# Stage one of a Strassen-style MoE layer: product 1 summed in product 0's PSUM bank, and the products in the order 0, 5, 1, 6, 3, 4, 2

## The chip, the cores and the metric

The program runs on one core of a Trainium2 chip. The metric is the device time of the whole program in microseconds (us). The core has engines that each work through their own list of instructions in order: TensorE (PE, with its weight loads listed apart as PEld), VectorE (DVE), ScalarE (ACT) and GpSimd (POOL); SyncE (SP) here only issues DMA transfers. They meet through semaphores: an instruction that must wait for another engine holds up everything behind it on its own engine.

## The reference

Sparse attention comes first, then a layer of 8 dense experts on its output:

```python
    B, H, S, D = attn_out.shape                      # 4, 8, 768, 64
    x = np.ascontiguousarray(attn_out.transpose(0, 2, 1, 3)).reshape(B * S, H * D)
...
    N, D = x.shape                                   # 3072, 512
    E = w_gate.shape[1]                              # 8
    logits = x @ w_gate
    logits = logits - logits.max()
    P = np.exp(logits)
    for _ in range(8):
        P /= P.sum(1, keepdims=True) + 1e-09
        P /= P.sum(0, keepdims=True) + 1e-09
        P *= N / E
    out = np.zeros((N, D), dtype=np.float32)
    for e in range(E):
        h = np.maximum(x @ w1[e], 0.0)               # w1[e]: 512 x 1024
        ye = h @ w2[e]                               # w2[e]: 1024 x 512
        out += P[:, e:e + 1] * ye
```

The attention masks blocks of 32 keys, takes exp and sum of each row of scores and multiplies by V. The change touches only `x @ w1[e]`.

## The kernel before

The attention fills about the first 420 us. From there on the kernel works through 32 items, one for each pair of an expert e and a batch b of 768 tokens (i = 4e + b). An item has two stages.

**Stage one** (`stage1(i, qi)`) computes relu(x w1) by a Strassen-like scheme: the two token halves (384 tokens), the two halves of the inner dimension and the two halves of F give four blocks of output, and seven products of prepared sums of blocks take the place of eight. An item has four units, qi = 0 to 3, each 128 rows of F in each half; there are 128 units in all. A product is six matmuls of 128x384 in f16 (two K tiles, each as high x high, high x low, low x high, so that the weights of its third matmul are the first that are read from the low half), and they accumulate in one PSUM bank, `p0` to `p6`, of a pool `ps_h` with four banks. `HDOWN` takes out a scale.

In a unit the products came in the order 0, 1, 5, 6, 3, 4, 2:

- Product 0 is copied to SBUF as `a1` by ScalarE (L1247).
- `comb` (L1212) is a VectorE operation that reads one product from PSUM and adds an SBUF tile: `r11` = product 1 + `a1`, then `a1` += product 5, `u3` = product 6 + `a1`, `c21` = product 3 + `u3`, `u3` += product 4, `a1` += product 4, and `a1` += product 2. Those are seven `comb` in a unit.
- ScalarE makes the relu of `r11` in place (L1252), of `u3` (L1272), of `a1` (L1277) and of `c21` (L1285).
- GpSimd makes the sums that stage two needs as its operands: `s1` = `a1` + `u3` (L1280), then three differences into `a1`, `r11` and `c21` (L1086).
- `emit` turns each of the seven operands into two f16 halves: the high one by ScalarE (L1221), the low one by VectorE or GpSimd (L1226, L1232), which waits for the high one. The pairs are the tiles `h`.

**Stage two** (`stage2(i, p)`, products in the order 1, 0, 5, 6, 3, 4, 2) has three steps for each of its seven products; a step is 12 matmuls of 128x256 (L1332, PSUM tile `py`) and a VectorE update of the output `acc` (L1356).

**What sets the order.** The main loop writes stage two of item i between the products of stage one of item i+1: three steps first, the other 18 spread over the 28 products, one step or none after each. `tick` tells a queue (`Slots`) what each piece costs, and the queue puts delayed work in between: the halves of `h`, the GpSimd sums, and the preparation of weights. A scheduler of the framework, which simulates the engines, then settles the order of each engine's list. Item 0's stage one has no stage two beside it.

**The switch of experts.** In the last unit of an expert's last batch (i = 3, 7, ... 27, qi = 3), every product, once it has been issued for the last time, starts the preparation of the next expert's weights in its place (`split_w1`, the `used` callback): ScalarE writes the high half (L1064), VectorE the low half (L1068). The seven weight tiles lie in the memory areas `arena` (products 0, 1, 5) and `attic` (6, 3, 4, 2), and the splits come in the order 0, 1, 6, 5, 3, 4, 2. The seven switches lie at about 641, 861, 1082, 1302, 1523, 1743 and 1963 us.

The loads of the next item's x (`load_x`) go out on SP for the products in the order 0, 1, 5, 6, 3, 4, 2, before and after the change. The changed function with what calls it, lines as in the profile of before:

Of the kernel before, what the change touches and what calls it, by code (L numbers as in the profile page):

```python
# [9 lines left out]
F32 = mybir.dt.float32  # L10
# [5 lines left out]
AF = mybir.ActivationFunctionType  # L16
# [4 lines left out]
P = 128  # L21
# [8 lines left out]
HDOWN = 2.0 ** -20  # L30
# [24 lines left out]
def tile_sparse_attention_moe(  # L55
# [11 lines left out]
    nc = tc.nc  # L67
    B, H, S, D = q.shape
    NT, DM = out.shape
    NE, _, FF = w1.shape  # L70
# [10 lines left out]
    KH = KD // 2  # L81
    FH = FF // 2
    CH = NC // 2
    TH = S // 2
# [866 lines left out]
    ps_h = mpool("ps_h", 4, space=PSUM)  # L951
# [133 lines left out]
    def sub(out, x, y):  # L1085
        nc.gpsimd.tensor_tensor(out=out, in0=x, in1=y, op=ALU.subtract)  # L1086
# [104 lines left out]
    def stage1(i, qi, used=None):  # L1191
        fs = slice(qi * P, (qi + 1) * P)
        lop = LOPE if i < NLE else LOP

        def product(p):
            slots.need(("w1", i // B, p))
            ps = ps_h.tile([P, 512], F32, tag="ph", name=f"p{p}_{i}_{qi}")[:, :TH]
            for kc in range(KH):
                for m, (l, r) in enumerate(((0, 0), (0, 1), (1, 0))):
                    nc.tensor.matmul(  # L1200
                        ps, lhsT=w1p[p][:, l, kc, fs], rhs=xp[p][:, r, kc],
                        start=(kc == 0 and m == 0), stop=(kc == KH - 1 and m == 2),
                    )
            if used and p in used:
                used[p]()
            return ps

        def fresh(nm):
            return upool.tile([P, TH], F32, tag="u", name=f"{nm}_{i}_{qi}")

        def comb(t, ps, other):
            nc.vector.scalar_tensor_tensor(  # L1212
                out=t, in0=ps, scalar=HDOWN, in1=other, op0=ALU.mult, op1=ALU.add
            )

        def emit(p, src, relu=False, delay=0):
            key = ("h", i, p), i, qi

            def high():
                h = hs[i, p, qi] = hfree.pop(0)  # L1220
                nc.scalar.activation(h[:, 0], src, AF.Relu if relu else AF.Copy)  # L1221

            def low():
                h = hs[i, p, qi]
                if relu:
                    nc.vector.scalar_tensor_tensor(  # L1226
                        out=h[:, 1], in0=src, scalar=0.0, in1=h[:, 0],
                        op0=ALU.max, op1=ALU.subtract,
                    )
                else:  # L1230
                    eng = nc.gpsimd if p in lop else nc.vector
                    eng.tensor_tensor(out=h[:, 1], in0=src, in1=h[:, 0], op=ALU.subtract)  # L1232

            if delay:
                slots.add(high, key, delay, act=0.52)
            else:
                high()
            if p in lop:
                slots.add(low, key, delay, pool=0.95)
            else:  # L1240
                slots.add(low, key, delay + 1, dve=0.6 if relu else 0.78)

        def tick(n, m):
            slots.tick(0.976, 0.55 * n, 0.5 * m)

        a1 = fresh("a1")
        nc.scalar.activation(a1, product(0), AF.Copy, scale=HDOWN)  # L1247
        tick(0, 1)
        yield
        r11 = fresh("r11")  # L1250
        comb(r11, product(1), a1)
        nc.scalar.activation(r11, r11, AF.Relu)  # L1252
        emit(0, r11)
        tick(1, 2)
        yield
        comb(a1, product(5), a1)
        tick(1, 0)
        yield
        u3 = fresh("u3")
        comb(u3, product(6), a1)  # L1260
        tick(1, 0)
        yield
        slots.settle(i, qi - 1)
        c21 = fresh("c21")
        comb(c21, product(3), u3)
        emit(1, c21, relu=True)
        tick(1, 1)
        yield
        p5 = product(4)
        comb(u3, p5, u3)  # L1270
        comb(a1, p5, a1)
        nc.scalar.activation(u3, u3, AF.Relu)  # L1272
        emit(3, u3)
        tick(2, 2)
        yield
        comb(a1, product(2), a1)
        nc.scalar.activation(a1, a1, AF.Relu)  # L1277

        def add():
            nc.gpsimd.tensor_tensor(out=s1, in0=a1, in1=u3, op=ALU.add)  # L1280
            sub(a1, a1, r11)
            slots.need((("h", i, 0), i, qi))
            sub(r11, s1, r11)
            slots.need((("h", i, 1), i, qi))
            nc.scalar.activation(c21, c21, AF.Relu)  # L1285
            sub(c21, c21, r11)

        s1 = fresh("s1")
        slots.add(add, (("sum", i), i, qi), 1, act=0.52, pool=4.3)
        emit(4, s1, delay=SD[0])  # L1290
        emit(6, a1, delay=SD[1])
        emit(5, r11, delay=SD[2])
        emit(2, c21, delay=SD[3])
        tick(1, 1)
        yield
# [94 lines left out]
    def run(steps):  # L1390
        for _ in steps:
            pass

    run(stage1(0, 0))
    for part in split_w2(0, wr[2]):
        part()
    for qi in range(1, FH // P):
        run(stage1(0, qi))
# [6 lines left out]
    def products(i):  # L1405
        e, b = divmod(i, B)
        for qi in range(FH // P):
            swap = qi == FH // P - 1 and b == B - 1 and e + 1 < NE
            yield from stage1(i, qi, split_w1(e + 1) if swap else None)
# [79 lines left out]
```

## Time and profile before

| what | value |
|---|---|
| median of 3 runs | 2212.83 us (2211.21 to 2213.3) |
| the profiled execution's own time | 2212.46 us |
| its span, first to last instruction | 2210.7 us |
| mean granted TensorE clock | 0.997 |
| PE busy | 2159.4 us (98%) |
| DVE busy | 1741.3 us (79%) |
| ACT busy | 1317.0 us (60%) |
| POOL busy | 1334.8 us (60%) |

The profile is one execution, recorded instruction by instruction. A row of the timeline has the start in us, the duration in us, the engine, the line of the kernel, the operation, the tile it writes and the tiles it reads (without the numbers in their names), the shape, and how many instructions run together; square brackets at its end give the idle time ahead of it on its engine and what ended that. Neighbouring matmuls overlap: the start of the next row, not the end of this one, says when the engine was free. The chain of waits follows the work that ended last back through what released it. The table of waits lists the idle time of an engine by what ended it: total us, number of times, longest.

### The profile page before, as it was taken

Reading aid. Unit: us, or ns where it says so; the run is one execution under the profiler, and the core shown is the slowest. Engines: PE = TensorE matmul, PEld = TensorE weight load, DVE = VectorE, ACT = ScalarE, POOL = GpSimd, SP = SyncE. Lnnn points to the kernel's source line nnn. Section 1 sums busy time; section 2 is a strip of 40 time slices with the busy share of each in tenths; the row PEclk is TensorE's granted clock in tenths of the full one; section 3 lists DMA queues with packets and bytes.
Section 4 is the critical chain, followed back from the end, with each engine's and each line's share of the span. In section 5 each row is a group of like instructions: output and inputs, shape, how many; then the busy total and the mean of one; then the engine's idle time right before and its main releaser. Section 6 shows DMA issues by size and latency. Waiting matters only on the chain.

```text
span 2210.7 us, 47146 instructions
## 1 busy us (share of the span) xinstructions
PE 2159.4 (98%) x18892; PEld 1599.2 (72%) x18892; DVE 1741.3 (79%) x2989; ACT 1317.0 (60%) x2443; POOL 1334.8 (60%) x1369
## 2 busy tenths in 40 slices
PE   6999999889999999999999999999999999999999
PEld 3777767657777777777777777777777777777777
DVE  7888999778877768876887688768876887688765
ACT  6988889765567556654565455545554555455442
POOL 3123455595578556855686568656865686567553
PEclk9999999999999999999999999999999999999999
DMA  7667866413121212121212121212121212121221
GB/s 169 139 134 160 210 124 145 128 65 118 51 89 51 89 51 89 51 89 51 89 51 89 51 89 51 89 51 89 51 89 51 89 51 89 51 89 58 79 79 51
DMA packets 195344, 192.35 MB, mean 87 GB/s; under 512 B 132124, under 2 KB 150580, under 8 KB 195124
## 3 DMA queue, kind: packets, MB, share of 16 engines
q1 hardware_dynamic: 194560, 189.30, 31.0%
q8 instruction: 148, 2.42, 0.4%
q14 instruction: 72, 0.59, 0.1%
q10 hardware_dynamic: 564, 0.03, 0.0%
HBM read 140.54 MB, written 17.30 MB: 71 GB/s over the span
## 4 chain that ended last, share of the span: by engine, by line
PE 77%; DVE 10%; ACT 4%; POOL 4%; issue 3%; DMA 1%; SPq 0%; DVEq 0%; POOLq 0%; ACTq 0%
PE py L1332 33%; PE p L1200 33%; PE u L760 3%; PE t L705 2%; PE t L702 2%; PE m L669 2%; PE m L672 2%; DVE top L678 2%; DVE a L1212 1%; DVE attic L1068 1%; POOL s L1280 1%; DVE h L1232 1%; DVE u L1212 1%; ACT h L1221 1%; DVE pl L721 1%
## 5 line engine op out<-in xcount | busy, mean ns | idle before, releaser
L1332 PE MATMUL py<-w2p,h 128*128 128x256 f16 x8064 | 972.9, 273 | 3.8 <-DVE h L1226 1.3
L1332 PEld LDWEIGHTS <-h 128*128 128x128 f16 x8064 | 788.8, 98 | 154.9 <-issue 3.2
L1232 POOL TENSOR_TENSOR h<-u,h 128x384 f16<-128x384 f32 x128 | 128.4, 1003 | 534.8 <-ACT h L1221 534.7
L1200 PE MATMUL p<-attic 128*128 128x384 f16 x2304 | 422.9, 327 | 8.4 <-DVE attic L1068 2.5
L1200 PEld LDWEIGHTS <-attic 128*128 128x128 f16 x3072 | 299.5, 98 | 178.3 <-issue 7.9
L1200 PE MATMUL p<-arena 128*128 128x384 f16 x2304 | 414.8, 326 | 1.4 <-DVE a L1212 0.9
L1356 DVE SCALAR_TENSOR_TENSOR acc<-py,spare,acc 128x256 f32<-128x256 f32 (+1 forms) x588 | 298.7, 514 | 98.6 <-PE py L1332 94.0
L1221 ACT ACTIVATE h<-c 128x384 f16<-128x384 f32 x256 | 131.5, 518 | 344.4 <-DVE c L1212 302.6
L1200 PEld LDWEIGHTS <-arena 128*128 128x128 f16 x2304 | 225.5, 98 | 126.5 <-issue 2.9
L1212 DVE SCALAR_TENSOR_TENSOR a<-p,a 128x384 f32<-128x384 f32 x384 | 211.1, 550 | 17.8 <-PE p L1200 5.0
L1232 DVE TENSOR_TENSOR h<-s,h 128x384 f16<-128x384 f32 x128 | 112.8, 881 | 135.4 <-ACT h L1221 135.3
L678 DVE TENSOR_REDUCE top<-m 128x1 f32<-128x768 f32 x192 | 181.8, 951 | 32.4 <-PE m L672 31.9
L710 ACT ACTIVATE pe<-t,qk 128x768 int32<-128x768 f32 x192 | 171.9, 898 | 46.3 <-PE t L705 43.3
L1086 POOL TENSOR_TENSOR c<-c,r 128x384 f32<-128x384 f32 x128 | 161.2, 1259 | 10.0
L1280 POOL TENSOR_TENSOR s<-a,u 128x384 f32<-128x384 f32 x128 | 138.1, 1079 | 37.0 <-ACT a L1277 36.2
L1086 POOL TENSOR_TENSOR r<-s,r 128x384 f32<-128x384 f32 x128 | 153.5, 1200 | 10.0
L1221 ACT ACTIVATE h<-r 128x384 f16<-128x384 f32 x256 | 128.0, 514 | 51.5 <-POOL r L1086 50.6
L1232 POOL TENSOR_TENSOR h<-r,h 128x384 f16<-128x384 f32 x128 | 146.4, 1144 | 2.6 <-ACT h L1221 2.0
L1200 PE MATMUL p<-arena,attic 128*128 128x384 f16 x768 | 146.4, 326 | 0.9 <-DVE a L1212 0.9
L669 PE MATMUL m<-kt,qt 128*128 128x512 f16 (+1 forms) x384 | 127.1, 331 | 9.3 <-DMA kt<-ks 6.8
L1086 POOL TENSOR_TENSOR a<-a,r 128x384 f32<-128x384 f32 x128 | 128.7, 1005 | 10.0
L702 PE MATMUL t<-qt,kt 128*128 128x512 f16 (+1 forms) x384 | 126.5, 329 | 6.2 <-DVE top L678 5.3
(205 smaller groups left out, 3635.3 us busy)
## 6 DMA issues: line engine op xcount, KB each, us to landing
arena<-xd SPq DMA_DIRECT2D x128, 384.0 KB, 3.4
attic<-xd SPq DMA_DIRECT2D x96, 384.0 KB, 3.6
r<-in_moe_w_dram SPq DMA_DIRECT2D x16, 2048.0 KB, 8.5
arena<-in_q_dram SPq DMA_DIRECT2D x16, 384.0 KB, 4.0
arena<-in_k_dram SPq DMA_DIRECT2D x16, 384.0 KB, 4.4
arena<-in_v_dram SPq DMA_DIRECT2D x4, 1536.0 KB, 8.1
xd<-xs_t SPq DMA_DIRECT2D x16, 384.0 KB, 3.1
out_dram<-acc SPq DMA_DIRECT2D x48, 128.0 KB, 1.7
```

The costliest lines, as they stand in the source:

```text
L669: nc.tensor.matmul(sc[:, lo:hi], lhsT=qt[:, 0, c], rhs=ka[:, lo:hi], start=True, stop=False)
L678: nc.vector.tensor_reduce(out=tops[n][:, c : c + 1], in_=sc[:, :S], axis=AX.X, op=ALU.max)
L702: nc.tensor.matmul(sc[:, lo:hi], lhsT=kt[:, 0, c], rhs=qa[:, lo:hi], start=True, stop=False)
L710: nc.scalar.activation(pe, sc[:, :S], AF.Exp, bias=EXP_SHIFT, scale=qk[n // 2][3])
L1086: nc.gpsimd.tensor_tensor(out=out, in0=x, in1=y, op=ALU.subtract)
L1200: nc.tensor.matmul(ps, lhsT=w1p[p][:, l, kc, fs], rhs=xp[p][:, r, kc], start=(kc == 0 and m == 0), stop=(kc == KH - 1 and m == 2),)
L1212: nc.vector.scalar_tensor_tensor(out=t, in0=ps, scalar=HDOWN, in1=other, op0=ALU.mult, op1=ALU.add)
L1221: nc.scalar.activation(h[:, 0], src, AF.Relu if relu else AF.Copy)
L1232: eng.tensor_tensor(out=h[:, 1], in0=src, in1=h[:, 0], op=ALU.subtract)
L1280: nc.gpsimd.tensor_tensor(out=s1, in0=a1, in1=u3, op=ALU.add)
L1332: nc.tensor.matmul(py, lhsT=hs[i, p, kc][:, l, tsl], rhs=w2p[p][:, r, kc], start=(old is None and kc == 0 and m == 0), stop=(kc == KF // 2 ...
L1356: nc.vector.scalar_tensor_tensor(out=dst, in0=src, scalar=c, in1=dst, op0=ALU.mult, op1=ALU.add)
```

## The change

```diff
-        def product(p):
+        def product(p, ps=None):
             slots.need(("w1", i // B, p))
-            ps = ps_h.tile([P, 512], F32, tag="ph", name=f"p{p}_{i}_{qi}")[:, :TH]
+            more = ps is not None
+            if not more:
+                ps = ps_h.tile([P, 512], F32, tag="ph", name=f"p{p}_{i}_{qi}")[:, :TH]
...
-                        start=(kc == 0 and m == 0), stop=(kc == KH - 1 and m == 2),
+                        start=(not more and kc == 0 and m == 0),
+                        stop=(kc == KH - 1 and m == 2),
+                        skip_group_check=True,
...
-        nc.scalar.activation(a1, product(0), AF.Copy, scale=HDOWN)
+        first = product(0)
+        nc.scalar.activation(a1, first, AF.Copy, scale=HDOWN)
         tick(0, 1)
-        yield
-        r11 = fresh("r11")
-        comb(r11, product(1), a1)
-        nc.scalar.activation(r11, r11, AF.Relu)
-        emit(0, r11)
-        tick(1, 2)
         yield
         comb(a1, product(5), a1)
         tick(1, 0)
+        yield
+        r11 = fresh("r11")
+        nc.scalar.activation(r11, product(1, first), AF.Relu, scale=HDOWN)
+        emit(0, r11)
+        tick(0, 2)
         yield
```

Product 1's six matmuls no longer start a bank of their own; they go on adding to product 0's bank, which ScalarE has copied to `a1` in the meantime. The copy must therefore be over before product 1's first matmul. ScalarE's relu of `r11` reads the sum from the bank with the scale `HDOWN`. A unit has six `comb` and takes six banks instead of seven. Product 5 comes second, product 1 third. The order in which the weights are split and the x loads go out is not edited. Lines after L1200 shift by two to seven: the matmul is L1202, `comb` L1216, the high half L1225, the copy L1252, the relu of `r11` L1259, the `acc` update L1360.

Since the framework's scheduler settles the lists anew, more moves than the diff says. The place shown here is the switch of experts, by the one into item 16 (at 1302 us before). In a row the line and operation are followed by the tile written and the tiles read: `h_25` is a pair of f16 halves, `attic_97` and `arena_93` are the memory areas of the weights, `r1_4` the raw w1 of expert 4, `p5_16_0` product 5 of item 16, unit 0; "waits" names the engine whose semaphore is waited for.

VectorE before, from the split of product 3's weights to that of product 2's:

```order
L1068 SCALAR_TENSOR_TENSOR attic_97<-r1_4_17198,sw1_4_17202,attic_97 128x1024
L1212 SCALAR_TENSOR_TENSOR r11_16_0_18555<-p1_16_0_18556,a1_16_0_18546 128x384 [waits PE_49,Activation_49]
L1356 SCALAR_TENSOR_TENSOR acc_3_9931<-py_15_0_0_18566,spare_6_16510,acc_3_9931 128x256 [waits DVE_49,PE_49]
L1232 TENSOR_TENSOR h_1_8073<-r11_16_0_18555,h_1_8073 128x384 [waits Activation_49]
L1212 SCALAR_TENSOR_TENSOR a1_16_0_18546<-p5_16_0_18581,a1_16_0_18546 128x384 [waits DVE_49,PE_49]
L1068 SCALAR_TENSOR_TENSOR attic_97<-r1_4_17198,sw1_4_17202,attic_97 128x1024
L1212 SCALAR_TENSOR_TENSOR u3_16_0_18591<-p6_16_0_18592,a1_16_0_18546 128x384 [waits DVE_49,PE_49]
L1356 SCALAR_TENSOR_TENSOR acc_3_9931<-py_15_0_1_18600,spare_6_16510,acc_3_9931 128x256 [waits PE_49]
L1068 SCALAR_TENSOR_TENSOR attic_97<-r1_4_17198,sw1_4_17202,attic_97 128x1024 [waits Activation_49]
```

VectorE now, the same stretch:

```order
L1068 SCALAR_TENSOR_TENSOR attic_97<-r1_4_17086,sw1_4_17090,attic_97 128x1024
L1236 TENSOR_TENSOR h_25_8097<-a1_15_3_18198,h_25_8097 128x384 [waits Activation_49]
L1216 SCALAR_TENSOR_TENSOR a1_16_0_18418<-p5_16_0_18429,a1_16_0_18418 128x384 [waits PE_49,Activation_49]
L1360 SCALAR_TENSOR_TENSOR acc_3_9924<-py_15_0_0_18437,spare_6_16406,acc_3_9924 128x256 [waits DVE_49,PE_49]
L1068 SCALAR_TENSOR_TENSOR attic_97<-r1_4_17086,sw1_4_17090,attic_97 128x1024 [waits Activation_49]
L1216 SCALAR_TENSOR_TENSOR u3_16_0_18461<-p6_16_0_18462,a1_16_0_18418 128x384 [waits DVE_49,PE_49]
L1068 SCALAR_TENSOR_TENSOR attic_97<-r1_4_17086,sw1_4_17090,attic_97 128x1024
L1236 TENSOR_TENSOR h_18_8090<-r11_16_0_18451,h_18_8090 128x384 [waits Activation_49]
```

The `comb` of `r11` and the low half of `r11`'s operand stood between the first two splits; the one is gone and the other now comes behind the third split. The low half `h_25`, which stood ahead of the first split, has gone behind it, and an `acc` update that stood ahead of the third split has gone.

ScalarE before, from the high halves of unit (15, 3) to the third split:

```order
L1221 ACTIVATE h_25_8097<-a1_15_3_18324 128x384 [waits Pool_49]
L1221 ACTIVATE h_18_8090<-r11_15_3_18355 128x384 [waits PE_49,Pool_49]
L1247 ACTIVATE a1_16_0_18546<-p0_16_0_18547 128x384 [waits PE_49]
L1221 ACTIVATE h_0_8072<-c21_15_3_18417 128x384 [waits Pool_49]
L1064 ACTIVATE attic_97<-r1_4_17198,sw1_4_17202 128x1024
L1252 ACTIVATE r11_16_0_18555<-r11_16_0_18555 128x384 [waits DVE_49]
L1221 ACTIVATE h_1_8073<-r11_16_0_18555 128x384 [waits Activation_49]
L1064 ACTIVATE attic_97<-r1_4_17198,sw1_4_17202 128x1024
```

ScalarE now:

```order
L1225 ACTIVATE h_25_8097<-a1_15_3_18198 128x384 [waits Pool_49]
L1252 ACTIVATE a1_16_0_18418<-p0_16_0_18419 128x384 [waits PE_49]
L1064 ACTIVATE attic_97<-r1_4_17086,sw1_4_17090 128x1024
L1225 ACTIVATE h_28_8100<-r11_15_3_18238 128x384 [waits Pool_49]
L1225 ACTIVATE h_7_8079<-c21_15_3_18289 128x384 [waits Pool_49]
L1064 ACTIVATE attic_97<-r1_4_17086,sw1_4_17090 128x1024
L1259 ACTIVATE r11_16_0_18451<-p0_16_0_18419 128x384 [waits PE_49]
L1225 ACTIVATE h_18_8090<-r11_16_0_18451 128x384 [waits Activation_49]
```

The copy of product 0 no longer stands behind the high half of the old unit's `r11`, both splits have moved ahead of the relu of the new `r11`, and that relu reads `p0_16_0`, which now holds the sum. On PE the unit's list at this place reads product 0, product 5, one stage-two step, five matmuls of product 6, product 1 on `p0_16_0` (its first matmul waits for ScalarE's copy), the last matmul of product 6, a step, product 3, a step, product 4 and product 2.

## The prediction

> **What bounds the kernel now.** I read the page first (busy shares, chain of waits), then the windows by stage, then PE's waits in the two stages, then the timeline at one switch and in item 0.
>
> ```profile
> PE 2159.4 (98%) x18892; PEld 1599.2 (72%) x18892; DVE 1741.3 (79%) x2989; ACT 1317.0 (60%) x2443; POOL 1334.8 (60%) x1369
> PE 77%; DVE 10%; ACT 4%; POOL 4%; issue 3%; DMA 1%; SPq 0%; DVEq 0%; POOLq 0%; ACTq 0%
> ```
>
> PE is busy 98% of the span, and the change leaves its number of matmuls alone. So VectorE's work can pay only where PE waits. The windows (length, then PE, PEld, DVE, ACT, POOL busy, granted clock, DMA share, GB/s) say where that is:
>
> ```profile
> 420.00:465.00 45.00, 38.18 (x288) 23.02 (x286) 34.32 (x61) 31.70 (x69) 27.99 (x24) 0.96 0.37 128
> 465.00:560.00 95.00, 88.99 (x738) 66.61 (x738) 74.27 (x134) 53.68 (x108) 67.32 (x63) 1.00 0.20 69
> 560.00:2184.00 1624.00, 1619.50 (x12402) 1212.08 (x12401) 1254.01 (x2157) 879.47 (x1777) 1063.43 (x995) 1.00 0.23 70
> ```
>
> PE idles 6.8 us in item 0's stage one (420 to 465), 6.0 us in the next 95 us, and only 4.5 us in the 1624 us that follow. These waits of PE are listed (total us, times, longest), first from 560 to 2184, then the largest from 420 to 560:
>
> ```profile
> PE p L1200 <- DVE attic L1068: 2.5, 6, 0.5
> PE cs L1169 <- DVE spare L1163: 0.6, 1, 0.6
> PE p L1200 <- ACT a L1247: 0.5, 1, 0.5
> ```
>
> ```profile
> PE p L1200 <- DVE a L1212: 4.0, 5, 2.2
> ...
> PE p L1200 <- ACT a L1247: 1.3, 1, 1.3
> PE p L1200 <- DVE r L1212: 1.1, 1, 1.1
> ```
>
> Late, six waits are for VectorE's split of weights, one at each switch of experts but one (the switch at 861 us waits for ScalarE's copy instead). Early, it is VectorE's `comb` that PE waits for. The rest of the kernel can give nothing.
>
> **What goes and stays, off the path.**
>
> ```profile
> L1212 DVE SCALAR_TENSOR_TENSOR r<-p,a 128x384 f32<-128x384 f32 x128 | 70.2, 549 | 41.0 <-ACT a L1247 23.1 <-PE p L1200 16.1 <-ACT h L1221 1.8
> L1252 ACT ACTIVATE r<-r 128x384 f32<-128x384 f32 x128 | 66.4, 519 | 39.6 <-DVE r L1212 39.5
> L1247 ACT ACTIVATE a<-p 128x384 f32<-128x384 f32 x128 | 61.4, 479 | 42.8 <-PE p L1200 42.7
> ```
>
> VectorE loses 128 `comb` of 549 ns, 70.2 us, 4% of its work. ScalarE's relu now reads PSUM; the copy that does so takes 479 ns against 519, so about 128 x 0.04 = 5 us less there. Both vanish behind PE: 70 us of VectorE is the cover and is worth nothing by itself. No matmul is added or removed: stage two already lets products 5, 6 and 2 add to an older bank, so I price the missing start at nothing.
>
> **The switches.** The timeline of PE into item 16:
>
> ```profile
> 1302.28 2.11 PE L1200 MATMUL p<-arena 128*128 128x384 f16 x12
> 1304.23 1.47 PE L1332 MATMUL py<-w2p,h 128*128 128x256 f16 x12
> 1305.54 1.14 PE L1200 MATMUL p<-arena 128*128 128x384 f16 x6
> 1306.51 1.14 PE L1200 MATMUL p<-arena,attic 128*128 128x384 f16 x6
> ...
> 1311.08 0.49 PE L1200 MATMUL p<-attic 128*128 128x384 f16 x2
> 1311.99 1.15 PE L1200 MATMUL p<-attic 128*128 128x384 f16 x6 [0.42 <-DVE attic L1068]
> 1312.97 0.93 PE L1332 MATMUL py<-w2p,h 128*128 128x256 f16 x7
> 1314.04 0.82 PE L1200 MATMUL p<-attic 128*128 128x384 f16 x4
> ```
>
> Twelve matmuls of 128x384 go from 1302.28 to 1304.23, 0.163 us each; twelve of 128x256 to 1305.54, 0.109 each. At that pace product 4's third matmul was due at 1311.08 + 0.33 = 1311.41 and came at 1311.99: 0.58 late. Product 2's third was due at 1312.97 + 7 x 0.109 = 1313.73 and came at 1314.04: 0.31 late. A switch costs 0.89 us. VectorE at that time (split of product 5's weights first, then of 3's, 4's, 2's):
>
> ```profile
> 1301.26 1.27 DVE L1068 SCALAR_TENSOR_TENSOR arena<-r,sw,arena 128x1024 f16<-128x1024 f32 x1
> ...
> 1306.08 2.02 DVE L1068 SCALAR_TENSOR_TENSOR attic<-r,sw,attic 128x1024 f16<-128x1024 f32 x1
> 1308.02 0.55 DVE L1212 SCALAR_TENSOR_TENSOR r<-p,a 128x384 f32<-128x384 f32 x1
> ...
> 1309.71 0.56 DVE L1232 TENSOR_TENSOR h<-r,h 128x384 f16<-128x384 f32 x1 [0.75 <-ACT h L1221]
> ...
> 1310.66 1.27 DVE L1068 SCALAR_TENSOR_TENSOR attic<-r,sw,attic 128x1024 f16<-128x1024 f32 x1
> ```
>
> Between the split of 3 (over at 1308.02) and that of 4 (from 1310.66) lie 2.64 us, of which the `comb` of `r11` takes 0.47 to the next start, the wait for ScalarE's high half of `r11` 0.75, and its low half 0.48. All three leave this place. In their stead come `h_25` (about 0.5), the `comb` of `a1` and one `acc` update (0.47 and 0.40). If split 3 still starts at 1306.08, that of 4 starts about 1308.02 + 0.5 + 0.47 + 0.4 = 1309.4, and is over at 1310.7 (1.27 long) or 1311.4 (2.02 long, as split 3), against 1311.41. The `comb` of `u3` (0.47) and split 2 (1.27) then end at 1312.4 to 1313.2. On PE product 2 now follows product 4 at once, so its third matmul is due at 1311.41 + 6 x 0.163 = 1312.39. Split 3 may start up to 0.7 sooner, since `h_25` and an `acc` update ahead of it are behind it now. So at a switch 0.89 goes, and 0 to 0.8 comes back; I take 0.75 saved, because the typical split behind the first is 1.27. Six switches: **-4.5 us** (0 to -5.3). The one at 861 us stays: ScalarE was busy elsewhere there.
>
> Two covers must hold. Product 5 now follows product 0 and is due at its low weights at 1302.28 + 8 x 0.163 = 1303.58; their split ended at 1302.53, 1.05 us ahead, and what stands before it on VectorE is lighter. Product 1 must follow ScalarE's copy of product 0. Its place on PE is after product 5, a step and five matmuls of 6: 1302.28 + 12 x 0.163 + 1.31 + 5 x 0.163 = 1306.36. The copy stands behind the high halves of `s1` and `a1`, which wait for GpSimd:
>
> ```profile
> 1301.58 1.81 POOL L1280 TENSOR_TENSOR s<-a,u 128x384 f32<-128x384 f32 x1 [0.33 <-ACT a L1277]
> 1303.47 1.00 POOL L1086 TENSOR_TENSOR a<-a,r 128x384 f32<-128x384 f32 x1
> 1304.89 0.51 ACT L1221 ACTIVATE h<-a 128x384 f16<-128x384 f32 x1
> 1306.21 0.47 ACT L1247 ACTIVATE a<-p 128x384 f32<-128x384 f32 x1
> ```
>
> GpSimd's `a` is over at 1304.47. A split's high half now comes ahead of the relu of `a1` on ScalarE, which may push `s` by 0.2 to 0.6. Then `h<-a` 0.5 and the copy 0.5: over between 1305.5 and 1306.1. Cover 0.3 to 0.9 us: thin, but there. In an ordinary unit a step and a part of another lie between product 0 and product 1, at least 2.8 us, and ScalarE waited 42.7 us in all for PE ahead of 128 copies (the row of L1247 above), 0.33 each: mostly it stands ready. Behind ScalarE's wait for product 1 queue the high halves; they feed stage two of a later item, and hold up nothing near.
>
> SP's loads of x: product 1 is used last some 3 us later in a unit now, and product 5's load stands behind product 1's on SP.
>
> ```profile
> arena<-xd SPq DMA_DIRECT2D x128, 384.0 KB, 3.4
> ```
>
> A unit has 42 matmuls at 0.163 and 63 at 0.109 (21 steps of 12 in an item of four units), 13.7 us; from product 1's end (about 4.1 into the last unit) to product 5 of the next (about 1 into it) are 10.6 us, two loads in a row take 6.8. No cost.
>
> **Item 0.** PE and VectorE where the largest early wait is:
>
> ```profile
> 450.24 2.08 PE L1200 MATMUL p<-attic 128*128 128x384 f16 x6 [2.22 <-DVE a L1212]
> ```
>
> ```profile
> 447.57 2.16 DVE L1232 TENSOR_TENSOR h<-a,h 128x384 f16<-128x384 f32 x1
> 449.65 0.54 DVE L1212 SCALAR_TENSOR_TENSOR a<-p,a 128x384 f32<-128x384 f32 x1
> ```
>
> ```profile
> 451.00:452.00 1.00, 1.00 (x5) 0.44 (x3) 1.00 (x3) 0.13 (x1) 1.00 (x1) 0.50 0.00 0
> ```
>
> PE waited for a bank that `comb` of product 5 had to read, and that stood behind two low halves, one of 2.16 us. In the new order it stands ahead of them. That wait of 2.2 us goes, and with it the half clock behind it: six matmuls took 1.88 us to the next start (452.12) instead of 0.98, and I count 1.4 us for the whole slow stretch (450 to 453, as an estimate from this row). The low halves still have to run, and ScalarE's copy is now something PE must wait for: I set against it one wait as the 1.3 us of the copy in the table. So 2.2 + 1.4 - 1.3 = **-2.3 us**. From both sides: all 4.0 + 1.1 + 1.4 gone, -6.5; or nothing gone and three more units that wait 1.3 for the copy, +3.9.
>
> The row shows a clock of 0.50 behind the wait. The Trainium skill ("TensorE: Matmul & The Clock Gate", Part 1: The HAM clock gate) says that the clock is halved after an idle window of about 3.4 us that runs freely, whatever the kernel does; by that rule the slow stretch might stay or go with the window's phase, and the sum would be 1.4 us less.
>
> **Sum.** -4.5 - 2.3 = -6.8 us. The profiled execution took 2212.46 us (1.76 around its span of 2210.7), so 2205.7; it lies 0.37 below the median of 2212.83, so I forecast **2206.0 us**. A measurement here can tell about 0.2%, 4.4 us, from no change.
>
> **Rivals.**
>
> *The waits only change their names (0.26).* At a switch ScalarE's high half, GpSimd's sums or the split itself stay late by as much as VectorE gains, and item 0 stays bound by the sum of VectorE and GpSimd work. For it: VectorE is 77% busy from 560 on and the split of 2 comes out within a few tenths of its due time by my own sum. Against: three of the pieces between the splits go. Half of each term: 2209.4; none: 2212.8.
>
> *ScalarE's copy holds up product 1 (0.10, slower).* PE may not add to the bank before the copy has read it, and the copy stands in ScalarE's list behind high halves that wait for GpSimd at 22 of the starts of items (by the new list). The cover at the switch is 0.3 to 0.9 us; the rival decides once the copy comes later than that. A stall of 0.5 us at 22 places and 3.9 in item 0, less the 4.5 of the switches, gives 11 + 3.9 - 4.5 = +10.4: 2223. Against it: the copies waited for PE, not the other way, in the row of L1247.
>
> The Trainium skill ("PSUM — Partial Sum Buffer", PSUM bank collisions raise a hardware error) says that two engines on the same bank at once are not arbitrated, so the order has to be kept by the program; no run here shows a collision, and the wait of product 1's first matmul for ScalarE in the new list agrees.
>
> **Chances and range.** The forecast 0.64, of which 0.06 comes out under 4.4 us; the first rival 0.26, the second 0.10, of which 0.01 stays under the bound. So faster 0.58, same 0.33, slower 0.09. The ends of the terms give -11.8 and, with the first rival, +3.9 (2201.0 and 2216.7). I leave out what needs both at their ends: 2201.5 to 2214.0.
>
> **What would show it.** Right: no `comb` into `r`, VectorE 70 us less busy; the six waits for `attic L1068` gone or under 0.2 us each; the 2.2 us wait in item 0 gone. Wrong: a wait of PE for ScalarE's L1252 with a count of 20 or more; waits for L1068 still about 0.4 us each; or a row of PE with DMA as releaser ahead of product 5.

## The result: slower by 0.3%, and the profile after

The changed kernel takes 2219.44 us (median of 7 runs, 2219.08 to 2221.92); the kernel before, run beside it, 2213.3 us (7 runs, 2211.21 to 2214.76). The ratio is 1.003 with a 95% interval of 1.002 to 1.004. The forecast of 2206.0 us had the wrong sign, and the time lies above the range that was given. The profiled execution of the changed kernel took 2219.44 us, 7.0 us more than that of before.

From the page of the changed kernel, busy times and the chain of waits:

```profile
PE 2160.8 (97%) x18892; PEld 1599.5 (72%) x18892; DVE 1660.6 (75%) x2861; ACT 1320.5 (60%) x2443; POOL 1336.8 (60%) x1369
PE 68%; DVE 12%; POOL 9%; ACT 6%; issue 4%; DMA 1%; SPq 0%; POOLq 0%; DVEq 0%; ACTq 0%
```

VectorE has the 128 operations less that were costed, and is 81 us less busy (70 were costed). Yet the chain that ended last now runs through GpSimd for 9% of the span (4% before). The windows, with the same columns as in the prediction:

```profile
420.00:465.00 45.00, 39.03 (x305) 23.52 (x305) 34.11 (x59) 32.85 (x72) 27.56 (x24) 1.00 0.40 136
465.00:560.00 95.00, 89.52 (x747) 67.44 (x746) 73.31 (x131) 51.20 (x104) 66.34 (x62) 1.00 0.21 69
560.00:2190.00 1630.00, 1619.21 (x12383) 1211.04 (x12382) 1174.25 (x2034) 884.39 (x1779) 1065.80 (x994) 1.00 0.23 70
```

Early, PE idles less (6.0 and 5.5 us against 6.8 and 6.0), and the half clock in item 0 is gone: 1.00 where 0.96 stood. From 560 us on PE idles 10.8 us where it idled 4.5. PE's waits there:

```profile
PE py L1336 <- DVE acc L1360: 8.5, 14, 0.9
PE p L1202 <- ACT a L1252: 1.4, 7, 0.2
PE cs L1169 <- DVE spare L1163: 0.9, 1, 0.9
```

The six waits for the split of w1 are gone. In their stead stage two waits 14 times, twice per expert, for VectorE's `acc` update, which must read a PSUM bank before the next step may use it. Product 1 waits for ScalarE's copy only seven times.

A sharper view is the pace: how far the starts of neighbouring matmuls lie apart beyond 0.163 us (128x384) and 0.109 us (128x256). Summed from 560 us on, over rows of the timeline that come more than 0.2 us late, that is 6.9 us before and 14.6 after; from 440 to 560 us, 14.5 before and 11.6 after. One expert, sixteen units, takes 220.4 us before and 221.5 after; from the fourth expert on these two repeat within 0.04 us. So 7 x 1.15 = 8 us are lost over the experts, and 2.4 us are won before them (from the end of the attention to the last unit of item 3). The end of the attention differs by 0.95 us between the two profiles (the last matmul of line 760 at 426.82 and 427.77); in all twelve profiles of this study it lies between 424.6 and 428.2, and that is scatter between executions.

**Where the new wait is.** It lies in the first unit of an expert's second batch, while w2 of the next expert is being split. There the scheduler's list has six stage-two steps in a row, before and after the change (before, a lone stage-one matmul stands behind the fourth). PE in the changed kernel, and below it VectorE:

```profile
1361.36 5.40 PE L1336 MATMUL py<-w2p,h 128*128 128x256 f16 x48
1367.60 2.78 PE L1336 MATMUL py<-w2p,h 128*128 128x256 f16 x24 [0.83 <-DVE acc L1360]
```

```profile
1367.08 1.65 DVE L1360 SCALAR_TENSOR_TENSOR acc<-py,spare,acc 128x256 f32<-128x256 f32 x4
```

Stage two has four banks. The burst fills them in 5.24 us (48 x 0.109), and the first `acc` update starts 5.72 us into it; 0.52 us after that start PE goes on. In the kernel before, the same burst starts at 1360.02, its fifth step 5.40 us and the first update 4.75 us later:

```profile
1364.77 1.65 DVE L1356 SCALAR_TENSOR_TENSOR acc<-py,spare,acc 128x256 f32<-128x256 f32 x4
```

```profile
1365.42 2.78 PE L1332 MATMUL py<-w2p,h 128*128 128x256 f16 x24
```

With the same 0.52 us the bank was free at 5.27, due at 5.40: the cover was 0.13 us, at this burst and at the other four of the last five (first update 4.73 to 4.75 us in). The lone matmul behind the fourth step is 0.16 us of it. No table of waits shows it, because a wait that does not happen is in none.

**Where the lateness comes from.** Following the releasers back, 24 us earlier, in the third unit of the first batch. ScalarE, VectorE and GpSimd of the changed kernel:

```profile
1336.70 0.52 ACT L1225 ACTIVATE h<-c 128x384 f16<-128x384 f32 x1
1337.13 0.47 ACT L1259 ACTIVATE r<-p 128x384 f32<-128x384 f32 x1
1337.63 0.52 ACT L1225 ACTIVATE h<-r 128x384 f16<-128x384 f32 x1
```

```profile
1338.19 0.64 DVE L1236 TENSOR_TENSOR h<-r,h 128x384 f16<-128x384 f32 x1 [0.96 <-ACT h L1225]
...
1339.14 0.54 DVE L1216 SCALAR_TENSOR_TENSOR c<-p,u 128x384 f32<-128x384 f32 x1
...
1341.14 0.55 DVE L1216 SCALAR_TENSOR_TENSOR u<-p,u 128x384 f32<-128x384 f32 x1
```

```profile
1342.88 0.92 POOL L1236 TENSOR_TENSOR h<-u,h 128x384 f16<-128x384 f32 x1 [4.47 <-ACT h L1225]
...
1358.06 1.00 POOL L1284 TENSOR_TENSOR s<-a,u 128x384 f32<-128x384 f32 x1
```

And VectorE and GpSimd of the kernel before in that unit:

```profile
1334.47 0.54 DVE L1232 TENSOR_TENSOR h<-r,h 128x384 f16<-128x384 f32 x1
...
1336.32 0.56 DVE L1212 SCALAR_TENSOR_TENSOR c<-p,u 128x384 f32<-128x384 f32 x1
...
1338.71 0.56 DVE L1212 SCALAR_TENSOR_TENSOR u<-p,u 128x384 f32<-128x384 f32 x1 [0.29 <-PE p L1200]
```

```profile
1340.46 0.91 POOL L1232 TENSOR_TENSOR h<-u,h 128x384 f16<-128x384 f32 x1 [3.80 <-ACT h L1221]
...
1355.76 0.99 POOL L1280 TENSOR_TENSOR s<-a,u 128x384 f32<-128x384 f32 x1
```

Before, the low half of `r11` was done when product 3 arrived. Now `r11` is made a product later; its high half on ScalarE comes behind the old unit's halves, and its low half stands in VectorE's list ahead of the sum of product 3 and waits 0.96 us there. Everything behind it is late. At the other end of the chain VectorE waits for the late `s` once more, by way of its high half on ScalarE. The changed kernel, then the kernel before:

```profile
1359.65 0.90 DVE L1236 TENSOR_TENSOR h<-s,h 128x384 f16<-128x384 f32 x1 [1.35 <-ACT h L1225]
```

```profile
1357.34 0.91 DVE L1232 TENSOR_TENSOR h<-s,h 128x384 f16<-128x384 f32 x1 [0.35 <-ACT h L1221]
```

From this row to the first `acc` update VectorE takes 7.43 us in both kernels. Counted from the start of the burst:

| step | before | after | low half of r11 held back (below) |
|---|---|---|---|
| sum of product 3 (`c`) | -23.70 | -22.22 | -23.71 |
| sum of product 4 (`u`) | -21.31 | -20.22 | -21.31 |
| GpSimd's low half of `u` | -19.56 | -18.48 | -19.57 |
| GpSimd's `s` of the next unit | -4.26 | -3.30 | -4.12 |
| VectorE's low half of that `s` | -2.68 | -1.71 | -2.54 |
| first `acc` update | +4.75 | +5.72 | +4.89 |

From the third of these steps to the fourth GpSimd has hardly a gap. Two windows show it, of the kernel before and of the changed one (GpSimd is the last busy time ahead of the clock, 14.69 us of 15.30 and 14.94 of 15.18):

```profile
1340.46:1355.76 15.30, 15.30 (x117) 11.25 (x115) 12.84 (x27) 7.66 (x15) 14.69 (x16) 1.00 0.62 179
```

```profile
1342.88:1358.06 15.18, 15.18 (x115) 11.06 (x114) 12.91 (x25) 7.74 (x15) 14.94 (x16) 1.00 0.63 182
```

The sums of the next w2 come on top of its work there, so the 1.1 us of the start are still 1 us at the end, and the wait is of that size. The pace shows 1.0 us at the burst, 0.6 + 0.15 at a second place, in the next unit (1383.01 and 1380.94), and 0.36 at the copy of the unit after that (1391.41): 2.1 us per expert, against 0.9 that the switch no longer costs.

### The profile page after: what moved, and what is told of

The parts are those of the page before. It is cut to its first block, busy times and chain, and to the rows that moved or that the text cites. A ratio compares the mean times of both kernels' runs of the same rounds, so it can differ in the third digit from the quotient of the medians.

```text
span 2217.7 us, 46842 instructions
## 1 busy us (share of the span) xinstructions
PE 2160.8 (97%) x18892; PEld 1599.5 (72%) x18892; DVE 1660.6 (75%) x2861; ACT 1320.5 (60%) x2443; POOL 1336.8 (60%) x1369
## 4 chain that ended last, share of the span: by engine, by line
PE 68%; DVE 12%; POOL 9%; ACT 6%; issue 4%; DMA 1%; SPq 0%; POOLq 0%; DVEq 0%; ACTq 0%
PE py L1336 30%; PE p L1202 28%; PE u L760 3%; POOL s L1284 2%; POOL r L1079 2%; DVE h L1236 2%; PE t L705 2%; PE t L702 2%; PE m L669 2%; PE m L672 2%; POOL h L1236 2%; DVE top L678 2%; ACT h L1225 1%; DVE acc L1360 1%; DVE w2p L1068 1%
## 5 line engine op out<-in xcount | busy, mean ns | idle before, releaser
L1336 PE MATMUL py<-w2p,h 128*128 128x256 f16 x8064 | 983.3, 273 | 13.7 <-DVE acc L1360 8.5
L1202 PE MATMUL p<-arena 128*128 128x384 f16 x2304 | 426.4, 326 | 4.3 <-ACT a L1252 2.5
L1236 POOL TENSOR_TENSOR h<-u,h 128x384 f16<-128x384 f32 x128 | 133.7, 1044 | 481.1 <-ACT h L1225 481.1
L1202 PE MATMUL p<-attic 128*128 128x384 f16 x2304 | 420.7, 326 | 2.9 <-DVE a L1216 2.9
L1202 PEld LDWEIGHTS <-attic 128*128 128x128 f16 x3072 | 300.2, 98 | 165.3 <-issue 4.3
L1360 DVE SCALAR_TENSOR_TENSOR acc<-py,spare,acc 128x256 f32<-128x256 f32 (+1 forms) x588 | 297.8, 513 | 117.9 <-PE py L1336 114.3
L1202 PEld LDWEIGHTS <-arena 128*128 128x128 f16 x2304 | 225.2, 98 | 128.0 <-issue 7.0
L1225 ACT ACTIVATE h<-c 128x384 f16<-128x384 f32 x256 | 133.0, 520 | 280.9 <-DVE c L1216 210.1
L1216 DVE SCALAR_TENSOR_TENSOR a<-p,a 128x384 f32<-128x384 f32 x384 | 210.8, 549 | 56.8 <-PE p L1202 33.5
L1225 ACT ACTIVATE h<-r 128x384 f16<-128x384 f32 x256 | 133.3, 521 | 77.6 <-POOL r L1086 73.8
L1086 POOL TENSOR_TENSOR c<-c,r 128x384 f32<-128x384 f32 x128 | 165.8, 1295 | 10.0
L1202 PE MATMUL p<-arena,attic 128*128 128x384 f16 x768 | 151.5, 326 | 0.1
L1236 DVE TENSOR_TENSOR h<-r,h 128x384 f16<-128x384 f32 x128 | 92.7, 724 | 74.4 <-ACT h L1225 74.0
L1225 ACT ACTIVATE h<-s 128x384 f16<-128x384 f32 x128 | 66.9, 523 | 136.4 <-POOL s L1284 136.4
L1236 DVE TENSOR_TENSOR h<-a,h 128x384 f16<-128x384 f32 x128 | 130.1, 1017 | 8.4 <-ACT h L1225 8.2
```

The source lines that it names most:

```text
L1202: nc.tensor.matmul(ps, lhsT=w1p[p][:, l, kc, fs], rhs=xp[p][:, r, kc], start=(not more and kc == 0 and m == 0), stop=(kc == KH - 1 and m = ...
L1216: nc.vector.scalar_tensor_tensor(out=t, in0=ps, scalar=HDOWN, in1=other, op0=ALU.mult, op1=ALU.add)
L1336: nc.tensor.matmul(py, lhsT=hs[i, p, kc][:, l, tsl], rhs=w2p[p][:, r, kc], start=(old is None and kc == 0 and m == 0), stop=(kc == KF // 2 ...
L1360: nc.vector.scalar_tensor_tensor(out=dst, in0=src, scalar=c, in1=dst, op0=ALU.mult, op1=ALU.add)
```

## The experiments

Theory A is the chain above (late `r11`, late GpSimd, no bank free). The rival is that the scheduler laid its lists badly for another reason, or that the missing VectorE work itself plays the part. Every time stands beside runs of the kernel before on the same chip (medians of 2212.7 to 2213.6 us). "Per expert" is the time from the relu of `a1` in one expert to the same in the next: 220.4 us before, 221.5 in the changed kernel.

**e1: the order alone.** From the kernel before:

```diff
+        second = product(5)
+        tick(0, 0)
+        yield
         r11 = fresh("r11")
         comb(r11, product(1), a1)
         nc.scalar.activation(r11, r11, AF.Relu)
         emit(0, r11)
-        tick(1, 2)
-        yield
-        comb(a1, product(5), a1)
-        tick(1, 0)
+        comb(a1, second, a1)
+        tick(2, 2)
         yield
```

> The products go 0, 5, 1, but product 1 keeps a bank of its own and the seventh VectorE sum makes r11 from it; VectorE has all its work of before. Theory A (late r11): in the changed kernel r11 is made third instead of second and its relu stands on ScalarE behind the high halves that wait for GpSimd, so the low half of r11 holds VectorE up ahead of the sum of product 3, u3 of the unit before the w2 split comes 1.1 us late, GpSimd, which is busy without a gap from there on, stays 1 us late, and the four-step burst of stage two finds no free bank (8.5 us of waits for acc). Here r11 comes no sooner, so the waits for acc stay (6 to 12 us) and the time is 2216 to 2223. Rival B (the lighter VectorE work, or the accumulation, made the scheduler lay the lists badly): the waits for acc are gone and the time is about before's, 2211 to 2215. Both: if the waits for the w1 split at the switches (2.5 us in before) are gone here too, it was the order and not the 70 us of VectorE work that removed them.

Measured: 2220.28 us, ratio 1.003 (1.0018 to 1.0042), 221.5 us per expert. PE's waits from 560 us on, the largest two:

```profile
PE p L1200 <- DVE r L1212: 3.4, 5, 0.7
PE py L1333 <- DVE acc L1357: 2.2, 6, 0.5
```

The order alone costs as much as the whole change, though not at the same places. The sum of product 3 is late here as well (1.52 us after the product's end in the unit shown above, 1.68 in the changed kernel, 0.20 before). But the expected 6 to 12 us of waits for `acc` did not come; a part sits at the switch, where product 4 waits for a bank that the sum of `r11` has to read (0.69 us at 1315.45) instead of for its split. So the order took the split's wait away only by putting another there. The run does more than change the order: VectorE's sum of product 5 must now follow that of `r11`, which it does not in the changed kernel.

**e2: VectorE makes the relu of r11.** From the changed kernel:

```diff
-        nc.scalar.activation(r11, product(1, first), AF.Relu, scale=HDOWN)
+        nc.vector.tensor_scalar(r11, product(1, first), HDOWN, 0.0, ALU.mult, ALU.max)
         emit(0, r11)
-        tick(0, 2)
+        tick(1, 1)
```

> The changed kernel, but VectorE and not ScalarE makes relu of r11 from the bank (scale and max in one operation); VectorE has as many operations as before the change. Theory A: r11 no longer waits in ScalarE's list for its relu, its high half comes 0.5 us sooner and with it the low half and u3; the waits for acc fall by about half, to 3 to 6 us, time 2213 to 2217. Rival B (lists laid badly): the lists stand in the same order as in the changed kernel, so nothing changes, 2218 to 2221. Rival C (VectorE's 70 us matter after all): slower than the changed kernel, 2221 or more, and the waits for the w1 split come back.

Measured: 2224.28 us, ratio 1.0051 (1.0039 to 1.0063), 222.0 us per expert.

```profile
PE py L1336 <- DVE acc L1360: 11.3, 7, 1.7
```

Theory A's guess for it was wrong in sign; the time is as rival C had it, but the waits for the split of w1 came back only twice (0.5 us). The sum of product 3 is as late (1.73 us after the product), so ScalarE's relu is not what makes it late; what e1, e2 and the changed kernel share is product 1's third place. The extra VectorE operation in the late stretch makes the first `acc` update another 0.9 us later (6.60 us into the burst, and 8.29 us instead of 7.43 from the low half of `s` on). One VectorE operation more is worth something there after all: 4.8 us between this kernel and the changed one, some 3 of them in the experts' period.

**e4: five banks for stage two, three for stage one.** From the changed kernel:

```diff
-    ps_h = mpool("ps_h", 4, space=PSUM)
-    ps_y = mpool("ps_y", 4, space=PSUM)
+    ps_h = mpool("ps_h", 3, space=PSUM)
+    ps_y = mpool("ps_y", 5, space=PSUM)
```

> The changed kernel with five PSUM banks for stage two and three for stage one's products. Theory A and its last link (no free bank in the burst): the fifth bank covers 1.31 us, more than the longest wait of 0.9, so the waits for acc are gone (under 1 us of 8.5); if three banks suffice for stage one, 2209 to 2213; if not, new waits of product matmuls for ScalarE's relu of r11 or for sums take some of it, up to 2225. Rival B: the waits stay, since VectorE is late whatever the banks.

Measured: 2221.74 us, ratio 1.0038 (1.0026 to 1.005), 221.8 us per expert.

```profile
PE py L1336 <- ACT w2p L1064: 7.9, 7, 1.3
PE p L1202 <- ACT a L1252: 4.7, 7, 0.7
```

The waits for `acc` are gone, as expected, and so the bank was the last link. But nothing is won: stage two now waits for ScalarE's high half of w2, 1.3 us an expert. That operation (1363.92) stands in ScalarE's list behind the high half of the same `s`, for which ScalarE had waited 2.51 us; so the lateness reaches the burst by another way. The waits for the copy grew too, from 1.4 to 4.7 us; what the bank taken from stage one adds to that was not run apart.

**e6: the low half of r11 held behind the sum of product 3, in every unit.** `not_earlier` is the kernel's own helper that keeps an instruction from moving ahead of its place. From the changed kernel:

```diff
-        emit(0, r11)
+        held = []
+        emit(0, r11, held=held)
...
         comb(c21, product(3), u3)
+        not_earlier(held[0])
         emit(1, c21, relu=True)
-        tick(1, 1)
+        tick(2, 1)
```

> The changed kernel, with the low half of r11 held in VectorE's list behind the sum of product 3 in every unit. Theory A: u3 of the unit before the w2 split comes about 1.1 us sooner, GpSimd too, and the first wait for acc (0.83 us in each of seven switches) goes, the second (0.43) shrinks; 8.5 us of waits fall to under 3; time 2209 to 2214. Rival B (another reason for the late burst: the w2 split itself or the order of GpSimd's list): the waits stay at 7 us or more, 2217 to 2221.

Measured: 2216.02 us (12 runs, 2212.21 to 2219.3), ratio 1.0013 (1.0004 to 1.0021), 220.8 us per expert. VectorE and GpSimd in the unit, then PE's waits:

```profile
1337.89 0.56 DVE L1216 SCALAR_TENSOR_TENSOR c<-p,u 128x384 f32<-128x384 f32 x1 [0.49 <-PE p L1202]
1338.37 0.55 DVE L1236 TENSOR_TENSOR h<-r,h 128x384 f16<-128x384 f32 x1
...
1340.29 0.56 DVE L1216 SCALAR_TENSOR_TENSOR u<-p,u 128x384 f32<-128x384 f32 x1 [0.29 <-PE p L1202]
```

```profile
PE p L1202 <- ACT a L1254: 3.4, 9, 1.5
PE py L1340 <- DVE acc L1364: 1.0, 2, 0.8
```

Now VectorE waits for PE and not for ScalarE, every step is back at its place of before within 0.14 us (the table's last column), and 8.5 us of waits for `acc` have become 1.0. The burst's stall by the pace falls from 1.0 to 0.18 us an expert. The mechanism is as theory A has it; the time is 2 us above what was expected, because this list has small waits at the switch (0.5 us by the pace) and one of 4.5 us for the split of w2 at 481 us. That last one is not due to the held halves alone: e9, in which nothing is held, has it too.

**e8: the same in one unit of an expert only** (`held = [] if i and i % B == 0 and qi == 2 else None`, the rest as in e6, and `tick(2 if held else 1, 1)`).

> The changed kernel, with the low half of r11 held behind the sum of product 3 only in the third unit of each expert's first batch (seven units). Theory A: the waits for acc fall from 8.5 us to about 1 as in the run where it is held everywhere, and the switches keep no wait for the w1 split; per expert 2.1 us of stalls become 0.8, so 9 us less than the changed kernel: 2209 to 2212, a little below before. Rival: the gain at this unit is paid back elsewhere, 2214 to 2217.

Measured: 2213.96 us (11 runs), ratio 1.0001 (0.9992 to 1.001), 220.6 us per expert.

```profile
PE py L1341 <- DVE acc L1365: 3.0, 7, 0.4
PE p L1202 <- ACT a L1254: 1.4, 7, 0.2
```

Seven low halves moved behind the sum of product 3 take back the loss, though the time is 2 us above what was expected. The burst's wait is gone (0.07 us by the pace), the switch keeps no wait. The second `acc` wait (0.59) and the copy (0.36) stayed, against the expectation. For the second one e6 shows the cause: there the low half of `r11` in that unit stands behind the sum of product 3 as well, takes 0.82 us instead of 1.28, and PE's stall at that place is 0.13 us. The wait for the copy is the same in e6 (0.36).

**e10: the kernel before with GpSimd 1 us late at that place.** One sum made twice in that unit, with the same result:

```diff
-            nc.gpsimd.tensor_tensor(out=s1, in0=a1, in1=u3, op=ALU.add)
+            for _ in range(2 if i and i % B == 0 and qi == 2 else 1):
+                nc.gpsimd.tensor_tensor(out=s1, in0=a1, in1=u3, op=ALU.add)
```

> The kernel before, with GpSimd's sum s1 made twice in the third unit of each expert's first batch: seven more operations of 1.0 us. Theory A (GpSimd is busy without a gap from that unit to the w2 split, and any lateness there reaches the burst of stage two): waits of PE for acc appear at the place where the changed kernel has them, 0.5 to 1.0 us and a second one of up to 0.6, seven times; the w1 waits of before stay; 2217 to 2224 with before at 2213. Rival (one us of lateness there is covered): no new waits, 2212 to 2215.

Measured: 2220.42 us, ratio 1.0032 (1.0019 to 1.0045), 221.4 us per expert.

```profile
PE py L1333 <- DVE acc L1357: 5.4, 7, 0.9
PE p L1200 <- DVE attic L1068: 2.6, 6, 0.5
```

Seven GpSimd operations of 1.0 us, on an engine that is 60% busy, cost the kernel before 7 to 8 us, as expected, and bring the same wait at the same place: the first `acc` update comes 5.78 us into the burst, 1.03 later than before. So 1 us of lateness there is enough for the wait, and by e6 and e8 the wait goes with the lateness.

**e7: the kernel before, with the low half held back at the switch** (`held = [] if i and i % B == 0 and qi == 0 else None`).

> The kernel before, with the low half of r11 held behind the sum of product 3 in VectorE's list, only in the first unit of an expert (the switch), seven units in all. Theory: in before it is this low half, waiting 0.75 us for ScalarE between the splits of product 3's and 4's weights, that makes PE wait at the switch; without it the two splits come about 1.2 us sooner and the waits for the w1 split (2.5 us listed, 0.89 us per switch by the pace) go: 6 us less at six or seven switches, time 2206 to 2209 with before at 2213. Rival (the sum of r11 itself and the work of VectorE are what delays the splits): half of the wait stays, 2210 to 2213.

Measured: 2212.37 us (11 runs), ratio 0.9998 (0.9989 to 1.0007), 220.3 us per expert.

```profile
1313.30 0.82 PE L1200 MATMUL p<-attic 128*128 128x384 f16 x4 [0.67 <-DVE attic L1068]
```

Missed. Product 4's split is in time now, but the scheduler put product 2 straight behind product 4, without a step between, so its split was due 1.3 us sooner; one stall of 0.83 us replaces two of 0.89 in all, and the listed waits for the split rise from 2.5 to 4.4 us. That the low half is the cause at the switch is not shown by this.

**e9: product 1 written right behind product 0, still on its bank** (0, 1, 5, 6, 3, 4, 2).

> The changed kernel with product 1 right behind product 0 (0, 1, 5, 6, 3, 4, 2), still on its bank. PE must wait for ScalarE's copy in each of the 128 units unless other matmuls can be put between: copy 0.47 us and the way there, 0.7 to 1.2 us each, 90 to 150 us in all if nothing lies between, 2300 to 2370; if the scheduler's list has a stage-two step between them (1.31 us) most of it is covered, 2225 to 2260. It prices the wait that the order 0, 5, 1 avoids.

Measured: 2215.64 us (8 runs), ratio 1.0016 (1.0006 to 1.0026), 220.9 us per expert.

```profile
PE py L1336 <- DVE acc L1360: 5.3, 7, 0.9
PE py L1336 <- DVE w2p L1068: 1.5, 5, 0.3
```

Far off: no wait for the copy is left in this stretch. The scheduler moves product 1 back by itself: in the unit shown above the second product starts at 1330.61, before the copy is over (1331.01), so it can't be product 1. What the code's order still changes is when the queue of delayed work is asked (`tick`). So this does not price the wait for the copy, which was not measured.

**e11 and e12: e9 with the low half held back** in the third unit of a first batch (e11), and in every unit but the first of each expert (e12).

> The kernel of the run with product 1 written right behind product 0, with the low half of r11 held behind the sum of product 3 only in the third unit of each expert's first batch. Theory A: the one late unit is put right, so the wait of the burst for acc (5.3 us in seven) and the one for the w2 split in it (1.5 us) go, and no other wait of that list stands in their place: 1.0 to 1.5 us less per expert than the 2215.6 of that run, 2206 to 2209, faster than before by over 0.2%. Rival (the gain is paid back at another wait, as in the run that held it in the changed kernel): 2211 to 2214.

Measured for e11: 2210.02 us (12 runs; one of 5828.73 us is left out of the ratio, and without it the median is 2209.93), ratio 0.9989 (0.998 to 0.9997), 220.0 us per expert: 1 us above what theory A expected, and below before by less than 0.2%. A burst stall of 0.5 us is left from the third switch on, which points to more than one late unit in this list.

> The same with the low half of r11 held behind the sum of product 3 in every unit but the first of an expert. Theory A: the waits of the burst go as well, 2206 to 2210 unless the many moved halves make other units late. Rival: holding it everywhere changes the scheduler's list in the early items, which costs 2 to 5 us there (as the 4.7 us wait for the w2 split at 481 us in the run that held it everywhere), 2210 to 2214.

Measured for e12: 2209.15 us (11 runs, 2205.93 to 2211.98), ratio 0.998 (0.9972 to 0.9989), 219.5 us per expert. All of PE's waits from 560 us on:

```profile
PE p L1202 <- ACT a L1254: 1.6, 2, 1.1
PE py L1341 <- DVE acc L1365: 0.8, 1, 0.8
PE cs L1169 <- DVE spare L1163: 0.4, 1, 0.4
```

By the pace 3.5 us of stalls are left from 560 us on, where the kernel before has 6.9 and the changed one 14.6; those left come before 900 us. This is the best version: 0.2% below the kernel before and 0.5% below the changed one. The accumulation is worth having once its late half is out of the way; what the kernel before would gain from halves held back in every unit was not run.

## Why the prediction was wrong

- **The bound, right as far as it went.** "The rest of the kernel can give nothing" is true of gains. The step from there to the sum left out that the rest can take: 1624 us with 4.5 us of idle PE hold a cover of 0.13 us at a burst of each switch from the third on, a place for which the prediction has no term.
- **The step that failed:** "Behind ScalarE's wait for product 1 queue the high halves; they feed stage two of a later item, and hold up nothing near." The high half of `r11` is waited for by its own low half, which stands in VectorE's list ahead of the sum of product 3, and through it by `u3`, GpSimd and the burst. Price: 2.1 us an expert. Of these the 1.0 at the burst is shown by e8 to be due to the low half in one unit (and by e10 to be what 1 us of lateness on GpSimd costs), and e6 shows the second `acc` wait, 0.6, to shrink to 0.13 when the low half in another unit is held back. The 0.15 ahead of it stays in e6, unexplained. The 0.36 at the copy stays in e6 and e8; it is the second rival's wait, behind a late `s` (last section). At that place e12 has none of it.
- **The switches, right in size, and in part by luck:** -4.5 us was forecast, and 0.89 at each of six, 5.3 us, has gone. But the forecast shortened the stretch between the splits of products 3 and 4 from 2.64 to 1.4 us, and it is 2.56: `h_25` takes 1.27 to the next start instead of 0.5, and the split of 4 waits 0.36 for ScalarE. What saved the time is that the split of 3 starts 1.07 us sooner, 2.73 us into the unit (which PE begins at 1304.52) instead of 3.80, where up to 0.7 was allowed for, and runs 1.62 instead of 2.02. In the changed kernel the splits of products 4 and 2 end in time:

```profile
1307.25 1.62 DVE L1068 SCALAR_TENSOR_TENSOR attic<-r,sw,attic 128x1024 f16<-128x1024 f32 x1
1308.80 1.34 DVE L1236 TENSOR_TENSOR h<-a,h 128x384 f16<-128x384 f32 x1
...
1311.36 1.52 DVE L1068 SCALAR_TENSOR_TENSOR attic<-r,sw,attic 128x1024 f16<-128x1024 f32 x1 [0.36 <-ACT attic L1064]
...
1313.27 1.27 DVE L1068 SCALAR_TENSOR_TENSOR attic<-r,sw,attic 128x1024 f16<-128x1024 f32 x1
```

```profile
1313.33 2.11 PE L1202 MATMUL p<-attic 128*128 128x384 f16 x12
```

  Product 4 reads its low weights at 1313.66, product 2 at 1314.63; the splits end at 1312.88 and 1314.54, 0.78 and 0.09 us ahead.
- **Item 0, right in size:** -2.3 was forecast, and 2.4 us were won before the experts (14.5 - 11.6 = 2.9 us less stall from 440 to 560). The wait of 2.2 us is gone and the clock stays at 1.00, as forecast. What takes a part back is not the copy (two waits, 1.1 us, where before had one of 1.3) but a new wait of 1.6 us for one of VectorE's sums into `u3` and 2.1 us, in three waits, for the split of w2.
- **VectorE's 70 us "worth nothing by itself", doubtful:** one operation of `r11` put back on VectorE costs 4.8 us by e2, some 3 of it in the experts, where VectorE is late already. What it was worth in the kernel before was not measured.
- **The rival of ScalarE's copy, a real wait of the wrong size:** 11 + 3.9 us were priced, 1.4 us (2.5 by the pace) came from 560 us on. At the switch its cover held, with 1.1 us (the copy ends at 1307.45, product 1 starts at 1308.59). The reading "0.33 each: mostly it stands ready" was an average: the 42.7 us that ScalarE waited in the kernel before lie ahead of 43 of the 128 copies.
- **The sum:** -6 at the switches (the 0.7 at 861 us went too), -2.4 early and +13 to 14 at the new waits, which is most of the measured +6; the forecast had the first two and, but for the copy, no row for the third.

## What to carry to other kernels

When work is moved off an engine that is not the bound, follow the moved value to every instruction that waits for it, and then ask what stands behind those in their engines' lists: an operation that only feeds something far away can still hold up what is near. Look for the stretches with the thinnest cover (a burst on PE, an engine with no gap for 15 us), for they turn 1 us of lateness into a wait, though no table of waits names them before. With a scheduler in between, fix the one instruction that is late rather than add buffers; here a fifth bank, taken from stage one, only moved the wait.

## What the runs showed of the hardware

Where a VectorE operation with two SBUF inputs and a GpSimd operation overlap in these rows, the one that starts second takes longer by about the time that the first still has to run. The split of weights takes 1.27 us with GpSimd idle (the row at 1313.27) and took 2.02 where it started during GpSimd's work (at 1306.08, a row of the prediction; a GpSimd sum ran from 1305.82 to 1307.02). GpSimd's `s`, 1.00 us at 1358.06, took 2.07 when it started 0.05 us behind such a split. VectorE and GpSimd of the changed kernel:

```profile
1388.31 1.27 DVE L1068 SCALAR_TENSOR_TENSOR w2p<-r,sw,w2p 128x1024 f16<-128x1024 f32 x1
```

```profile
1388.36 2.07 POOL L1284 TENSOR_TENSOR s<-a,u 128x384 f32<-128x384 f32 x1
```

The excess of 1.07 us is close to the 1.22 us that the split still had to run. The Trainium skill ("SBUF — State Buffer", Who interferes with whom) says that a VectorE instruction with two SBUF inputs contends with a GpSimd instruction that reads SBUF, and that one with at most one SBUF input, outside the two-port modes, does not. These rows agree with the first part, though no run here was made to test it; the second part no row here shows. It matters for this case: that late `s` is what ScalarE's copy of product 0 stands behind where product 1 waits.

The half clock came back in e6 behind its wait of 4.5 us at 481 us, for about 6 us:

```profile
485.00:488.00 3.00, 2.13 (x11) 1.52 (x11) 3.00 (x4) 0.00 (x0) 2.92 (x2) 0.50 0.00 0
488.00:491.00 3.00, 3.00 (x16) 2.14 (x15) 3.00 (x6) 2.49 (x5) 0.61 (x1) 0.50 0.03 5
```

A granted clock of 0.50 raises the price of such a wait: 4.5 us and some 2.7 us behind it (26 matmuls at 0.104 us over their pace).
